# One ring of seven PSUM banks, a step over three quads and new evictors in a windowed-attention backward kernel

## The chip, the cores and the metric

The kernel runs on one core of one Trainium2 chip. The metric is device time in microseconds (us), median of several executions. Executions of one kernel agree within about 0.3%. Runs 1 to 8 were on one chip and 9 to 14 on another; the kernel before took 2572 to 2573 us on both.

PE is TensorE's matmuls, PEld its weight loads, DVE is VectorE, ACT is ScalarE, POOL is GpSimd, SP is SyncE. A "quad" is four tiles of 128 tokens (two 8x8 windows each); there are 128 quads. A "period" is the time between the scores of one quad and of the next.

## The reference, cut

```python
xw  = windows(x)                       # 1024 windows of 64 tokens, C = 384
qkv = xw @ wqkv
p   = softmax(q @ k.T * C ** -0.5)     # 64x64 per window
out = (p @ v) @ wo
# returned: out, and the gradients to x, wqkv, wo for a given grad_out; all bfloat16
```

The kernel folds the weights in pairs first (A, AT for q and k, B, BT for v and wo), so that per quad it needs: two projections z (from grad_out) and y (from x), the scores `sd`, softmax and its backward pass (`Pb`, `Sb`), products u and v, transposes of y and z back to token order (`yq`, `zq`), transposes of Pb and Sb ("turn": `PT`, `ST`), per tile an "attention" of six 64x64-block products (po, pd, pu, pw), and the weight gradients, which sum x-transposed times U and W over all tiles ("GF").

## The kernel before

Every product goes to a PSUM bank and is copied ("evicted") to SBUF by DVE or ACT. Eight banks are in use, in four pools:

```python
ps_pj = tile_pool(name="ps_pj", bufs=2, PSUM)   # z, y, u, v, yz transposes, turns
ps_sd = tile_pool(name="ps_sd", bufs=1, PSUM)   # scores
ps_at = tile_pool(name="ps_at", bufs=4, PSUM)   # po, pd, pu, pw of one attention
ps_dw = tile_pool(name="ps_dw", bufs=1, PSUM)   # a weight gradient, open for 12 matmuls
...
def uv(st, t, part):                            # u: evicted by DVE, v: by ACT
    wgt, dst, cp = ((B_sb, st["uq"], nc.vector.tensor_copy), (AT_sb, st["vq"], nc.scalar.copy))[part]
    pj = ps_pj.tile([P, C], F32, tag="pj")
    for m in range(CK):
        nc.tensor.matmul(pj[:], lhsT=st["xT"][:, t, m, :], rhs=wgt[:, m, :], ...)
    cp(out=dst[:, t, :], in_=pj[:])
...
def attend(st, t):                              # po, pu, pd evicted by ACT, pw by DVE
    both((po, "PT", "uq", True, True), (pd, "Pb", "zq", True, False))
    nc.scalar.copy(out=osb[:], in_=po[:])
    nc.sync.dma_start(out=dram_tile(out_0, bp, t0 + t), in_=osb[:])
    both((pu, "ST", "xq", True, True), (pd, "Sb", "yq", False, False))
    nc.scalar.copy(out=st["Uq"][:, t, :], in_=pu[:])
    both((pw, "Pb", "dq", True, True), (pd, "ST", "vq", False, True))
    nc.vector.tensor_copy(out=st["Wq"][:, t, :], in_=pw[:])
    nc.scalar.copy(out=dsb[:], in_=pd[:])
...
def step(a, b):                 # a: the quad projected now; b: the quad before, attended now
    A(project, 0, 0); A(project, 0, 1); B(0); A(project, 0, 2); A(project, 1, 0); B(1)
    A(project, 1, 1); A(project, 1, 2)
    filler(8)                   # weight-gradient matmuls, one by one
    A(scores); A(soft, 0); A(soft, 1)
    filler(4)
    A(uv, 0, 0); A(uv, 0, 1); A(soft, 2); A(uv, 1, 0); A(uv, 1, 1); A(soft, 3)
    B(2)
    A(uv, 2, 0); A(uv, 2, 1); A(soft, 4); A(uv, 3, 0); A(uv, 3, 1)
    filler(4)
    A(soft, 5)
    for t in range(QUAD):
        A(yz_tok, t, 0); filler(1); A(yz_tok, t, 1); filler(1)
    B(3)
    A(turn, 0); A(turn, 1)
```

PE, DVE and ACT execute in this program order; SP and POOL (the DMA queues) are placed by the scheduler.

Of the kernel before, what the change touches and what calls it, by code (L numbers as in the profile page):

```python
# [9 lines left out]
ALU = mybir.AluOpType  # L10
# [8 lines left out]
MANUAL = {mybir.EngineType.PE, mybir.EngineType.DVE, mybir.EngineType.Activation}  # L19
# [3 lines left out]
def kernel(  # L23
# [36 lines left out]
    ps_pj = ctx.enter_context(tc.tile_pool(name="ps_pj", bufs=2, space=bass.MemoryType.PSUM))  # L60
    ps_sd = ctx.enter_context(tc.tile_pool(name="ps_sd", bufs=1, space=bass.MemoryType.PSUM))
    ps_at = ctx.enter_context(tc.tile_pool(name="ps_at", bufs=4, space=bass.MemoryType.PSUM))
    ps_dw = ctx.enter_context(tc.tile_pool(name="ps_dw", bufs=1, space=bass.MemoryType.PSUM))
# [10 lines left out]
    for jm in range(JK):  # L74
        pt = ps_pj.tile([P, C], BF16, tag="pj")
        for m in range(CK):
            nc.tensor.transpose(pt[:, m * P:(m + 1) * P], w_sb[:, m, jm * P:(jm + 1) * P], ident[:])
        nc.vector.tensor_copy(out=wT_sb[:, jm, :], in_=pt[:])
    woT_sb = const.tile([P, CK, C], BF16)
    for mo in range(CK):  # L80
        pt = ps_pj.tile([P, C], BF16, tag="pj")
# [8 lines left out]
    for dst, left, lo, right, ro, sc in (  # L90
# [5 lines left out]
        for mr in range(CK):  # L96
            pc = ps_pj.tile([P, C], F32, tag="pj")
# [16 lines left out]
    def load(st):  # L114
        bp, t0 = st["at"]
        st["xq"] = xq = grp.tile([P, QUAD, C], BF16, tag="xq", name="xq", bufs=2 * GQ + 3)
        st["dq"] = dq = qp.tile([P, QUAD, C], BF16, tag="dq", name="dq", bufs=4)
# [8 lines left out]

    def project(st, kind, mo):
# [5 lines left out]
        pj = ps_pj.tile([P, QUAD, 2, WT], F32, tag="pj")  # L133
# [3 lines left out]
        if kind == 0:  # L137
            nc.scalar.copy(out=yz[:, mo, :, 0:4:3, :], in_=pj[:])  # L138
            nc.vector.tensor_copy(out=st["zc"][:, mo, :, :, :], in_=yz[:, mo, :, 0:4:3, :])  # L139
        else:  # L140
            nc.scalar.copy(out=yz[:, mo, :, 1:3, :], in_=pj[:])  # L141
# [50 lines left out]
    def uv(st, t, part):  # L192
# [3 lines left out]
        wgt, dst, cp = ((B_sb, st["uq"], nc.vector.tensor_copy), (AT_sb, st["vq"], nc.scalar.copy))[part]  # L196
        pj = ps_pj.tile([P, C], F32, tag="pj")
# [5 lines left out]
    def yz_tok(st, t, part):  # L203
        src, dst = ((st["yz"][:, :, t, 1:3, :], st["yq"]), (st["zc"][:, :, t, :, :], st["zq"]))[part]
        pt = ps_pj.tile([P, CK, P], BF16, tag="pj")
# [4 lines left out]
    def turn(st, kind):  # L210
        src, n = ((st["Pb"], "PT"), (st["Sb"], "ST"))[kind]
        st[n] = dst = qp.tile([P, QUAD, WT], BF16, tag=n, name=n)
        pt = ps_pj.tile([P, QUAD, WT], BF16, tag="pj")
# [5 lines left out]
    def attend(st, t):  # L219
# [4 lines left out]
        po = ps_at.tile([P, C], F32, tag="at", name="po")  # L224
        pd = ps_at.tile([P, C], F32, tag="at", name="pd")
        pu = ps_at.tile([P, C], F32, tag="at", name="pu")
        pw = ps_at.tile([P, C], F32, tag="at", name="pw")
# [8 lines left out]
        nc.scalar.copy(out=osb[:], in_=po[:])  # L236
        nc.sync.dma_start(out=dram_tile(out_0, bp, t0 + t), in_=osb[:])
        both((pu, "ST", "xq", True, True), (pd, "Sb", "yq", False, False))
        nc.scalar.copy(out=st["Uq"][:, t, :], in_=pu[:])  # L239
        both((pw, "Pb", "dq", True, True), (pd, "ST", "vq", False, True))  # L240
        nc.vector.tensor_copy(out=st["Wq"][:, t, :], in_=pw[:])  # L241
        dsb = ob.tile([P, C], BF16, tag="d")
        nc.scalar.copy(out=dsb[:], in_=pd[:])  # L243
        for h, w in ((LO, 1), (HI, 0)):
            nc.gpsimd.dma_start(out=dram_tile(out_1, bp, t0 + t)[WIN * w:WIN * (w + 1)], in_=dsb[h, :])  # L245

    fill = []

    def gf_group(sts):
        def one(f, ma):  # L250
            n = len(sts) * QUAD
            pw = None
            for i in range(n):
                if i == 0:
                    pw = ps_dw.tile([P, C], F32, tag="dw")
                st, t = sts[i // QUAD], i % QUAD
                nc.tensor.matmul(pw[:], lhsT=st["xq"][:, t, ma * P:(ma + 1) * P],  # L257
                                 rhs=st["UW"[f] + "q"][:, t, :], start=(i == 0), stop=(i == n - 1))
                if i == n - 1:
                    nc.vector.tensor_tensor(out=GF_acc[:, f, ma, :], in0=pw[:], in1=GF_acc[:, f, ma, :], op=ALU.add)  # L260
                yield
        for f in range(2):
            for ma in range(CK):
                yield from one(f, ma)
# [9 lines left out]
    def step(a, b):  # L274

        A = (lambda f, *r: f(a, *r)) if a is not None else (lambda f, *r: None)
        B = (lambda t: attend(b, t)) if b is not None else (lambda t: None)
        A(project, 0, 0)
        A(project, 0, 1)
        B(0)  # L280
        A(project, 0, 2)
        A(project, 1, 0)
        B(1)
        A(project, 1, 1)
        A(project, 1, 2)
        filler(8)
        A(scores)
        A(soft, 0)
        A(soft, 1)
        filler(4)  # L290
        A(uv, 0, 0)
        A(uv, 0, 1)
        A(soft, 2)
        A(uv, 1, 0)
        A(uv, 1, 1)
        A(soft, 3)
        B(2)
        A(uv, 2, 0)
        A(uv, 2, 1)
        A(soft, 4)  # L300
        A(uv, 3, 0)
        A(uv, 3, 1)
        filler(4)
        A(soft, 5)
        for t in range(QUAD):
            A(yz_tok, t, 0)
            filler(1)
            A(yz_tok, t, 1)
            filler(1)
        B(3)  # L310
        A(turn, 0)
        A(turn, 1)

    quads = [(bp, t0) for bp in range(NBP) for t0 in range(0, NT, QUAD)]
    sts = [{"at": q, "i": i} for i, q in enumerate(quads)]
    AHEAD = 2
    with tc.manual_schedule(engines=MANUAL):
        for i in range(min(AHEAD, len(sts))):
            load(sts[i])
        held = []  # L320
        for i in range(len(sts) + 1):
            if i + AHEAD < len(sts):
                load(sts[i + AHEAD])
            step(sts[i] if i < len(sts) else None, sts[i - 1] if i else None)
            if i:
                held.append(sts[i - 1])
                sts[i - 1] = None
            if held and (len(held) == GQ or i == len(sts)):
# [6 lines left out]
    for f in range(2):  # L335
        nc.vector.tensor_copy(out=GFb[:, f, :, :], in_=GF_acc[:, f, :, :])
        for mb in range(CK):
            pt = ps_pj.tile([P, C], BF16, tag="pj")
# [53 lines left out]
```

## Time and profile before

| | before |
|---|---|
| time | 2573.8 us |
| period | 19.65 us, 128 of them, plus 59 us of start and end |
| PE / DVE / ACT busy | 90% / 68% / 50% |
| PE idle | 256 us |
| chain of waits: PE / DVE | 47% / 49% |

The page of the kernel before: busy microseconds and share of the span, then the chain that ended last, as shares of the span by engine and by line.

```profile
PE 2318.2 (90%) x22910; PEld 1259.7 (49%) x22910; DVE 1751.3 (68%) x4515; ACT 1295.4 (50%) x2957; POOL 862.0 (33%) x1542
...
DVE 49%; PE 47%; issue 2%; ACT 0%; DMA 0%; SPq 0%; ACTq 0%
```

PE looks full, but the chain runs over DVE for half of its length. The timeline of PE in one period of the kernel before (start, duration, line, tile, count, and in brackets the idle time before it and what ended that):

```profile
1224.80 0.65 PE L199 MATMUL pj<-B_sb,xT 128*128 128x384 bf16 x3
1225.28 0.65 PE L199 MATMUL pj<-AT_sb,xT 128*128 128x384 bf16 x3
1226.50 0.65 PE L199 MATMUL pj<-B_sb,xT 128*128 128x384 bf16 x3 [0.57 <-ACT vq L201]
...
1230.71 0.81 PE L257 MATMUL pw<-Uq,xq 128*128 128x384 bf16 x4
...
1232.60 0.33 PE L207 MATMUL pt<-ident,yz 128*128 128x128 bf16 x3 [0.34 <-DVE yq L208]
...
1235.42 0.29 PE L216 MATMUL pt<-ident,Pb 64*64 64x64 bf16 x8
1235.54 0.30 PE L216 MATMUL pt<-ident,Sb 64*64 64x64 bf16 x8
1236.47 1.46 PE L135 MATMUL pj<-dT,BT_sb 128*128 128x512 bf16 x6 [0.64 <-DVE PT L217]
```

Read the starts, not the durations. The first two u/v products start 0.48 us apart, three matmuls each. The third starts 1.22 us after the second: 0.73 us lost, of which the bracket shows only 0.57, since the modelled end of a matmul lies 0.16 us after the start of the next one. Four such places, and smaller ones, make up the 3 us by which the period exceeds the sum of PE's start-to-start pitches (16.6 us). The Trainium skill ("Perfetto Trace Analysis", Identifying Performance Opportunities) says that the same bubble repeated on the engine that should be saturated can mean that there is not enough SBUF or PSUM for the next tile; here the bubbles repeat in every period.

### The profile page before, as it was taken

Reading aid. Unit: us, or ns where it says so; the run is one execution under the profiler, and the core shown is the slowest. Engines: PE = TensorE matmul, PEld = TensorE weight load, DVE = VectorE, ACT = ScalarE, POOL = GpSimd, SP = SyncE. Lnnn points to the kernel's source line nnn. Section 1 sums busy time; section 2 is a strip of 40 time slices with the busy share of each in tenths; the row PEclk is TensorE's granted clock in tenths of the full one; section 3 lists DMA queues with packets and bytes.
Section 4 is the critical chain, followed back from the end, with each engine's and each line's share of the span. In section 5 each row is a group of like instructions: output and inputs, shape, how many; then the busy total and the mean of one; then the engine's idle time right before and its main releaser. Section 6 shows DMA issues by size and latency. Waiting matters only on the chain.

```text
span 2574.3 us, 59437 instructions
## 1 busy us (share of the span) xinstructions
PE 2318.2 (90%) x22910; PEld 1259.7 (49%) x22910; DVE 1751.3 (68%) x4515; ACT 1295.4 (50%) x2957; POOL 862.0 (33%) x1542
## 2 busy tenths in 40 slices
PE   7899999999999999999999999999999999999997
PEld 4444544444444545444444445444444445454444
DVE  5676677667667766776676677667666766776674
ACT  3545554545555455545455554555454455545552
POOL 2333333333333333333333333333333333333321
PEclk9999999999999999999999999999999999999999
DMA  7455555655555555555555555555555555555531
GB/s 176 101 121 118 122 118 119 129 133 118 118 123 118 121 119 124 115 120 131 129 122 117 122 119 121 121 124 114 124 130 127 121 117 124 116 119 123 122 90 47
DMA packets 624477, 308.61 MB, mean 120 GB/s; under 512 B 458816, under 2 KB 607040, under 8 KB 624192
## 3 DMA queue, kind: packets, MB, share of 16 engines
q1 hardware_dynamic: 550064, 203.49, 37.9%
q0 software_dynamic: 73728, 101.02, 15.4%
q8 instruction: 179, 2.93, 0.5%
q14 instruction: 106, 0.87, 0.1%
q10 hardware_dynamic: 400, 0.29, 0.0%
HBM read 101.84 MB, written 101.84 MB: 79 GB/s over the span
## 4 chain that ended last, share of the span: by engine, by line
DVE 49%; PE 47%; issue 2%; ACT 0%; DMA 0%; SPq 0%; ACTq 0%
PE pj L135 21%; DVE uq L201 10%; PE pw L257 10%; PE pt L207 6%; DVE GF_acc L260 5%; DVE Wq L241 5%; DVE sh L167 4%; DVE mx L162 4%; DVE pr L183 4%; PE sd L149 4%; DVE yq L208 3%; PE po L232 3%; DVE Sb L190 2%; DVE Pb L179 2%; DVE D L185 2%
## 5 line engine op out<-in xcount | busy, mean ns | idle before, releaser
L245 POOL DMA_DIRECT2D out_dram<-dsb x1024 | 586.4, 577 | 1056.1 <-ACT dsb L243 1032.0
L201 ACT CAST vq<-pj 128x384 bf16<-128x384 f32 x512 | 245.3, 479 | 615.9 <-PE pj L199 607.4
L236 ACT CAST osb<-po 128x384 bf16<-128x384 f32 x512 | 255.0, 498 | 508.2 <-PE po L232 500.2
L120 POOL DMA_DIRECT2D dq<-in_grad_out_dram x512 | 276.2, 544 | 624.8 <-PE pt L216 610.6
L199 PEld LDWEIGHTS <-xT 128*128 128x128 bf16 x3072 | 287.5, 97 | 389.7 <-issue 231.7
L199 PE MATMUL pj<-B_sb,xT 128*128 128x384 bf16 x1536 | 333.7, 325 | 93.0 <-ACT vq L201 72.5
L257 PE MATMUL pw<-Wq,xq 128*128 128x384 bf16 x1536 | 384.4, 326 | 2.2 <-DVE GF_acc L260 2.1
L135 PE MATMUL pj<-dT,BT_sb 128*128 128x512 bf16 x1152 | 293.4, 381 | 80.2 <-DVE PT L217 79.9
L257 PEld LDWEIGHTS <-xq 128*128 128x128 bf16 x3072 | 291.0, 98 | 137.2 <-issue 6.3
L162 DVE TENSOR_REDUCE mx<-sd 64x4 f32<-64x256 f32 x256 | 108.2, 422 | 361.7 <-PE sd L149 357.7
L199 PE MATMUL pj<-AT_sb,xT 128*128 128x384 bf16 x1536 | 332.7, 325 | 12.2 <-DVE uq L201 1.1
L257 PE MATMUL pw<-Uq,xq 128*128 128x384 bf16 x1536 | 339.1, 326 | 1.9 <-DVE GF_acc L260 1.9
L139 DVE COPY zc<-yz 128x512 bf16<-128x512 bf16 x384 | 113.1, 295 | 329.2 <-ACT yz L138 329.2
L241 DVE CAST Wq<-pw 128x384 bf16<-128x384 f32 x512 | 283.8, 554 | 18.4 <-PE pw L232 3.6
L135 PE MATMUL pj<-xT,A_sb 128*128 128x512 bf16 x1152 | 291.8, 380 | 0.0
L201 DVE CAST uq<-pj 128x384 bf16<-128x384 f32 x512 | 284.1, 556 | 4.3
L138 ACT CAST yz<-pj 128x512 bf16<-128x512 f32 x384 | 230.4, 600 | 106.4 <-PE pj L135 98.5
L243 ACT CAST dsb<-pd 128x384 bf16<-128x384 f32 x512 | 266.9, 521 | 0.0
L239 ACT CAST Uq<-pu 128x384 bf16<-128x384 f32 x512 | 260.5, 509 | 0.0
L141 ACT CAST yz<-pj 128x512 bf16<-128x512 f32 x384 | 232.9, 677 | 0.4 <-PE pj L135 0.2
L207 PE MATMUL pt<-ident,yz 128*128 128x128 bf16 x1536 | 168.1, 217 | 49.1 <-DVE yq L208 46.9
L208 DVE COPY yq<-pt 128x384 bf16<-128x384 bf16 x512 | 182.0, 356 | 43.1 <-PE pt L207 21.1
(71 smaller groups left out, 3391.1 us busy)
## 6 DMA issues: line engine op xcount, KB each, us to landing
xq<-in_x_dram SPq DMA_DIRECT2D x512, 96.0 KB, 2.9
dq<-in_grad_out_dram POOLq DMA_DIRECT2D x512, 96.0 KB, 2.5
out_dram<-dsb POOLq DMA_DIRECT2D x1024, 48.0 KB, 2.2
out_dram<-osb SPq DMA_DIRECT2D x512, 96.0 KB, 2.8
xT<-xq SPq DMA_TRANSPOSE x128, 3.9
dT<-dq SPq DMA_TRANSPOSE x128, 4.3
w_sb<-in_wqkv_dram SPq DMA_DIRECT2D x1, 864.0 KB, 5.9
out_dram<-dw_sb SPq DMA_DIRECT2D x1, 864.0 KB, 3.8
```

The lines of the kernel that those rows point to most:

```text
L120: nc.gpsimd.dma_start(out=dq[:, t, :], in_=dram_tile(grad_out, bp, t0 + t))
L135: nc.tensor.matmul(pj[:].rearrange("p t w k -> p (t w k)"), lhsT=wgt[:, m, mo * P:(mo + 1) * P], rhs=src[:, :, m, :], start=(m == 0), stop ...
L199: nc.tensor.matmul(pj[:], lhsT=st["xT"][:, t, m, :], rhs=wgt[:, m, :], start=(m == 0), stop=(m == CK - 1))
L201: cp(out=dst[:, t, :], in_=pj[:])
L207: nc.tensor.transpose(pt[:, m, :], src[:, m, :, :].rearrange("p w k -> p (w k)"), ident[:])
L208: nc.vector.tensor_copy(out=dst[:, t, :].rearrange("p (m c) -> p m c", m=CK), in_=pt[:])
L236: nc.scalar.copy(out=osb[:], in_=po[:])
L239: nc.scalar.copy(out=st["Uq"][:, t, :], in_=pu[:])
L241: nc.vector.tensor_copy(out=st["Wq"][:, t, :], in_=pw[:])
L243: nc.scalar.copy(out=dsb[:], in_=pd[:])
L245: nc.gpsimd.dma_start(out=dram_tile(out_1, bp, t0 + t)[WIN * w:WIN * (w + 1)], in_=dsb[h, :])
L257: nc.tensor.matmul(pw[:], lhsT=st["xq"][:, t, ma * P:(ma + 1) * P], rhs=st["UW"[f] + "q"][:, t, :], start=(i == 0), stop=(i == n - 1))
```

## The change

The intent: let no product wait for a bank, give DVE's softmax steps cover, and keep PE in long runs. It has six parts, all in one commit:

1. **Ring.** The pools of two, four and one banks become one pool of seven.
2. **Order.** A step spans three quads: scores and softmax of b, attention of the quad before (c), projection of the quad after (a).
3. **Pairs.** Attentions of tiles 0 and 1 run back to back, so do those of 2 and 3.
4. **Blocks.** Weight gradients run as two blocks of twelve matmuls a step and no longer fill gaps one by one.
5. **Evictors.** u goes from DVE to ACT, U from ACT to DVE, two of three y from ACT to DVE.
6. **Queues.** SP and POOL issue in program order, and grad_out has five buffers instead of four.

```diff
-MANUAL = {PE, DVE, Activation}
+MANUAL = {SP, Pool, PE, DVE, Activation}
-    ps_pj = ... bufs=2   ;   ps_at = ... bufs=4   ;   ps_dw = ... bufs=1
+    ring = ctx.enter_context(tc.tile_pool(name="ring", bufs=7, space=bass.MemoryType.PSUM))
@@ step, cut @@
+        B(scores)
+        B(soft, 0)
+        B(uv, 0, 0)
+        B(uv, 0, 1)
+        B(soft, 1)
+        B(uv, 1, 0)
+        B(uv, 1, 1)
+        B(soft, 2)
+        C_(attend, 0)
+        B(soft, 3)
+        C_(attend, 1)
+        B(soft, 4)
+        filler(1)                      # now a block of twelve matmuls
+        B(uv, 2, 0)
+        B(uv, 2, 1)
+        B(soft, 5)
+        B(uv, 3, 0)
+        B(uv, 3, 1)
+        for t in range(QUAD):
+            B(yz_tok, t, 0)
+            B(yz_tok, t, 1)
+        C_(attend, 2)
+        C_(attend, 3)
+        B(turn, 0)
+        B(turn, 1)
+        for kind in range(2):
+            for mo in range(CK):
+                A(project, kind, mo)
+        filler(1)
+    EV = {"z": "AAA", "y": "DAD", "u": "AAAA", "v": "AAAA", "o": "AAAA", "U": "DDDD", "W": "DDDD", "d": "AAAA"}
... (cut: every pool.tile(...) becomes ring.tile(..., tag="r"); copies go through EV)
```

More of the change, by code (lines that the diff above doesn't have):

```diff
@@ L18 @@
 QUAD = 4
-MANUAL = {mybir.EngineType.PE, mybir.EngineType.DVE, mybir.EngineType.Activation}
+MANUAL = {mybir.EngineType.SP, mybir.EngineType.Pool, mybir.EngineType.PE, mybir.EngineType.DVE, mybir.EngineType.Activation}
 @with_exitstack
@@ L59 @@
     ob = ctx.enter_context(tc.tile_pool(name="ob", bufs=3))
-    ps_pj = ctx.enter_context(tc.tile_pool(name="ps_pj", bufs=2, space=bass.MemoryType.PSUM))
     ps_sd = ctx.enter_context(tc.tile_pool(name="ps_sd", bufs=1, space=bass.MemoryType.PSUM))
-    ps_at = ctx.enter_context(tc.tile_pool(name="ps_at", bufs=4, space=bass.MemoryType.PSUM))
-    ps_dw = ctx.enter_context(tc.tile_pool(name="ps_dw", bufs=1, space=bass.MemoryType.PSUM))
+    ring = ctx.enter_context(tc.tile_pool(name="ring", bufs=7, space=bass.MemoryType.PSUM))
     ident = const.tile([P, P], BF16)
@@ L74 @@
     for jm in range(JK):
-        pt = ps_pj.tile([P, C], BF16, tag="pj")
+        pt = ring.tile([P, C], BF16, tag="r")
         for m in range(CK):
@@ L80 @@
     for mo in range(CK):
-        pt = ps_pj.tile([P, C], BF16, tag="pj")
+        pt = ring.tile([P, C], BF16, tag="r")
         for m in range(CK):
@@ L96 @@
         for mr in range(CK):
-            pc = ps_pj.tile([P, C], F32, tag="pj")
+            pc = ring.tile([P, C], F32, tag="r")
             for mc in range(CK):
@@ L116, in load @@
         st["xq"] = xq = grp.tile([P, QUAD, C], BF16, tag="xq", name="xq", bufs=2 * GQ + 3)
-        st["dq"] = dq = qp.tile([P, QUAD, C], BF16, tag="dq", name="dq", bufs=4)
+        st["dq"] = dq = qp.tile([P, QUAD, C], BF16, tag="dq", name="dq", bufs=5)
         for t in range(QUAD):
@@ L125, in load @@
                                         in_=src[:].rearrange("p t c -> p (t c)"))
+    ENG = {"D": nc.vector.tensor_copy, "A": nc.scalar.copy}
     def project(st, kind, mo):
@@ L132, in project @@
         wgt, src = ((BT_sb, st["dT"]), (A_sb, st["xT"]))[kind]
-        pj = ps_pj.tile([P, QUAD, 2, WT], F32, tag="pj")
+        pj = ring.tile([P, QUAD, 2, WT], F32, tag="r")
         for m in range(CK):
@@ L137, in project @@
         if kind == 0:
-            nc.scalar.copy(out=yz[:, mo, :, 0:4:3, :], in_=pj[:])
+            ENG[EV["z"][mo]](out=yz[:, mo, :, 0:4:3, :], in_=pj[:])
             nc.vector.tensor_copy(out=st["zc"][:, mo, :, :, :], in_=yz[:, mo, :, 0:4:3, :])
         else:
-            nc.scalar.copy(out=yz[:, mo, :, 1:3, :], in_=pj[:])
+            ENG[EV["y"][mo]](out=yz[:, mo, :, 1:3, :], in_=pj[:])
     def scores(st):
@@ L195, in uv @@
                 st[n] = qp.tile([P, QUAD, C], BF16, tag=n, name=n)
-        wgt, dst, cp = ((B_sb, st["uq"], nc.vector.tensor_copy), (AT_sb, st["vq"], nc.scalar.copy))[part]
-        pj = ps_pj.tile([P, C], F32, tag="pj")
+        wgt, dst, cp = ((B_sb, st["uq"], ENG[EV["u"][t]]), (AT_sb, st["vq"], ENG[EV["v"][t]]))[part]
+        pj = ring.tile([P, C], F32, tag="r")
         for m in range(CK):
@@ L204, in yz_tok @@
         src, dst = ((st["yz"][:, :, t, 1:3, :], st["yq"]), (st["zc"][:, :, t, :, :], st["zq"]))[part]
-        pt = ps_pj.tile([P, CK, P], BF16, tag="pj")
+        pt = ring.tile([P, CK, P], BF16, tag="r")
         for m in range(CK):
@@ L212, in turn @@
         st[n] = dst = qp.tile([P, QUAD, WT], BF16, tag=n, name=n)
-        pt = ps_pj.tile([P, QUAD, WT], BF16, tag="pj")
+        pt = ring.tile([P, QUAD, WT], BF16, tag="r")
         for t in range(QUAD):
@@ L223, in attend @@
             st["Wq"] = grp.tile([P, QUAD, C], BF16, tag="Wq", name="Wq")
-        po = ps_at.tile([P, C], F32, tag="at", name="po")
-        pd = ps_at.tile([P, C], F32, tag="at", name="pd")
-        pu = ps_at.tile([P, C], F32, tag="at", name="pu")
-        pw = ps_at.tile([P, C], F32, tag="at", name="pw")
+        po = ring.tile([P, C], F32, tag="r", name="po")
+        pd = ring.tile([P, C], F32, tag="r", name="pd")
+        pu = ring.tile([P, C], F32, tag="r", name="pu")
+        pw = ring.tile([P, C], F32, tag="r", name="pw")
         def both(straight, crossed):
@@ L235, in attend @@
         osb = ob.tile([P, C], BF16, tag="o")
-        nc.scalar.copy(out=osb[:], in_=po[:])
+        ENG[EV["o"][t]](out=osb[:], in_=po[:])
         nc.sync.dma_start(out=dram_tile(out_0, bp, t0 + t), in_=osb[:])
         both((pu, "ST", "xq", True, True), (pd, "Sb", "yq", False, False))
-        nc.scalar.copy(out=st["Uq"][:, t, :], in_=pu[:])
+        ENG[EV["U"][t]](out=st["Uq"][:, t, :], in_=pu[:])
         both((pw, "Pb", "dq", True, True), (pd, "ST", "vq", False, True))
-        nc.vector.tensor_copy(out=st["Wq"][:, t, :], in_=pw[:])
         dsb = ob.tile([P, C], BF16, tag="d")
-        nc.scalar.copy(out=dsb[:], in_=pd[:])
+        ENG[EV["d"][t]](out=dsb[:], in_=pd[:])
         for h, w in ((LO, 1), (HI, 0)):
             nc.gpsimd.dma_start(out=dram_tile(out_1, bp, t0 + t)[WIN * w:WIN * (w + 1)], in_=dsb[h, :])
+        ENG[EV["W"][t]](out=st["Wq"][:, t, :], in_=pw[:])
     fill = []
     def gf_group(sts):
-        def one(f, ma):
-            n = len(sts) * QUAD
-            pw = None
-            for i in range(n):
-                if i == 0:
-                    pw = ps_dw.tile([P, C], F32, tag="dw")
-                st, t = sts[i // QUAD], i % QUAD
-                nc.tensor.matmul(pw[:], lhsT=st["xq"][:, t, ma * P:(ma + 1) * P],
-                                 rhs=st["UW"[f] + "q"][:, t, :], start=(i == 0), stop=(i == n - 1))
-                if i == n - 1:
-                    nc.vector.tensor_tensor(out=GF_acc[:, f, ma, :], in0=pw[:], in1=GF_acc[:, f, ma, :], op=ALU.add)
-                yield
+        n = len(sts) * QUAD
         for f in range(2):
             for ma in range(CK):
-                yield from one(f, ma)
+                pw = ring.tile([P, C], F32, tag="r", name="pg")
+                for i in range(n):
+                    st, t = sts[i // QUAD], i % QUAD
+                    nc.tensor.matmul(pw[:], lhsT=st["xq"][:, t, ma * P:(ma + 1) * P],
+                                     rhs=st["UW"[f] + "q"][:, t, :], start=(i == 0), stop=(i == n - 1))
+                nc.vector.tensor_tensor(out=GF_acc[:, f, ma, :], in0=pw[:], in1=GF_acc[:, f, ma, :], op=ALU.add)
+                yield
     def filler(n):
@@ L272, in filler, with step, on @@
                 fill.pop(0)
-    def step(a, b):
-        A = (lambda f, *r: f(a, *r)) if a is not None else (lambda f, *r: None)
-        B = (lambda t: attend(b, t)) if b is not None else (lambda t: None)
-        A(project, 0, 0)
-        A(project, 0, 1)
-        B(0)
-        A(project, 0, 2)
-        A(project, 1, 0)
-        B(1)
-        A(project, 1, 1)
-        A(project, 1, 2)
-        filler(8)
-        A(scores)
-        A(soft, 0)
-        A(soft, 1)
-        filler(4)
-        A(uv, 0, 0)
-        A(uv, 0, 1)
-        A(soft, 2)
-        A(uv, 1, 0)
-        A(uv, 1, 1)
-        A(soft, 3)
-        B(2)
-        A(uv, 2, 0)
-        A(uv, 2, 1)
-        A(soft, 4)
-        A(uv, 3, 0)
-        A(uv, 3, 1)
-        filler(4)
-        A(soft, 5)
-        for t in range(QUAD):
-            A(yz_tok, t, 0)
-            filler(1)
-            A(yz_tok, t, 1)
-            filler(1)
-        B(3)
-        A(turn, 0)
-        A(turn, 1)
+    def step(c, b, a):
+        def on(st):
+            return (lambda f, *r: f(st, *r)) if st is not None else (lambda f, *r: None)
+        C_, B, A = on(c), on(b), on(a)
+        B(scores)
[16 more added lines that the diff above has]
+        B(uv, 3, 1)
+        for t in range(QUAD):
+            B(yz_tok, t, 0)
[8 more added lines that the diff above has]
+        filler(1)
@@ L314 @@
+    EV = {"z": "AAA", "y": "DAD", "u": "AAAA", "v": "AAAA", "o": "AAAA", "U": "DDDD", "W": "DDDD", "d": "AAAA"}
     quads = [(bp, t0) for bp in range(NBP) for t0 in range(0, NT, QUAD)]
     sts = [{"at": q, "i": i} for i, q in enumerate(quads)]
+    n = len(sts)
     AHEAD = 2
     with tc.manual_schedule(engines=MANUAL):
-        for i in range(min(AHEAD, len(sts))):
+        for i in range(min(AHEAD, n)):
             load(sts[i])
         held = []
-        for i in range(len(sts) + 1):
-            if i + AHEAD < len(sts):
+        get = lambda i: sts[i] if 0 <= i < n else None
+        for i in range(-1, n + 1):
+            if AHEAD <= i + AHEAD < n:
@@ L323 @@
                 load(sts[i + AHEAD])
-            step(sts[i] if i < len(sts) else None, sts[i - 1] if i else None)
-            if i:
+            step(get(i - 1), get(i), get(i + 1))
+            if i > 0:
                 held.append(sts[i - 1])
                 sts[i - 1] = None
-            if held and (len(held) == GQ or i == len(sts)):
+            if held and (len(held) == GQ or i == n):
                 fill.append(gf_group(held))
@@ L337 @@
         for mb in range(CK):
-            pt = ps_pj.tile([P, C], BF16, tag="pj")
+            pt = ring.tile([P, C], BF16, tag="r")
             for ma in range(CK):
@@ L344 @@
         for i, (lhs, f, rhs, r0) in enumerate(((GFT, 0, w_sb, C), (GFb, 0, w_sb, 0), (GFT, 1, woT_sb, 0))):
-            pe = ps_pj.tile([P, C], F32, tag="pj")
+            pe = ring.tile([P, C], F32, tag="r")
             for mb in range(CK):
@@ L355 @@
     for mc in range(CK):
-        pe = ps_pj.tile([P, C], F32, tag="pj")
+        pe = ring.tile([P, C], F32, tag="r")
         for ma in range(CK):
```

## The prediction

> **What bounds it now.** The timeline shows one period of 19.65 us per quad of tiles (128 of them), plus about 60 us of start and end. The page gives PE 90%, DVE 68%, ACT 50% busy, but the Trainium skill ("Trainium Kernel Development and Optimization", Performance Expectations) says that matmul busy time is a bad metric, as matmuls are pipelined. This trace agrees: a 128x384 matmul lasts 325 ns, yet they start 163 ns apart. From start-to-start pitches PE needs per quad: projections 18 x 0.217 = 3.9 us, u/v 3.9, weight gradients 3.9, attention 4 x 0.62 = 2.5, scores 0.70, y/z transposes 1.3, turns 0.25: about 16.6 us. So 3 us (15%) of each period is PE waiting. The chain of waits alternates, PE 47%, DVE 49%: scores -> softmax on DVE -> y/z copies -> turn -> next projection. By the timeline the stalls start-to-start are about 0.7 and 0.25 (u/v for the two "pj" banks, evicted behind exp or softmax work), 0.3 (u), 0.5+0.25 (transposes behind yq), 0.8 (projection behind PT), and about 0.08 at each change between full and 64x64 matmuls.
>
> **What the change does.** The instructions stay the same in number on PE; order and evictors move.
> - Two-deep "pj" + four "at" + one "dw" becomes one ring of 7; 42 allocations per step, exactly six turns. A product waits for the eviction seven products earlier instead of two.
> - Projections of the next quad and one 12-matmul block (3.9 + 1.95 us of PE) stand between turn and the next scores, so PT/ST are needed only by the next step's attention: the 0.8 us wait goes.
> - Four uq evictions move DVE->ACT, four Uq ACT->DVE (DVE about 0.555, ACT about 0.49 us each: nearly neutral), two of three y evictions ACT->DVE. A 128x512 on DVE is estimated at 0.69 us from 0.555 for 384 and its slope. DVE: 13.7 -> about 15 us per quad; ACT: 10.1 -> about 9.
> - SP and Pool issue in program order; loads still lead by over a step, so I expect no cost.
>
> **Walking the new order** with trace durations (DVE pitch 0.47, yq/zq 0.28, ACT 0.375, release to PE 0.05): u/v of t=0,1 unhindered; second attention waits about 0.4 us for osb (behind exp); block 0.1; attentions of t=2,3 about 0.5 in total behind the yq/zq copies; first projection 0.3 behind Wq (DVE backlog of four U/W). Sum about 1.4 us of stalls: period 18.0-18.2 us, DVE then over 80% busy. All 1.5 us is on the critical path, since PE/DVE alternate there.
>
> **Time:** 128 x 18.1 + 60 = about **2375 us** (7.7% less). Eight in ten: 2310 to 2450. Faster by over 2%: 0.90; within 2%: 0.08; slower: 0.02.
>
> **What would show it.** Period 18.1 us in the timeline; PE idle falls from 256 us to about 130; PE matmul durations unchanged; "pj <- PT" waits gone (80 us before), vq waits near zero (72 before), yq waits gone or moved to "po/pd <- zq"; DVE 75-80% of the span or more, ACT about 48%; chain more PE than before (over 60%), DVE share falling. New waits: pw <- ACT osb about 0.4 us a step, pj <- DVE Wq about 0.3.
>
> **What would make it wrong.** DVE is within 10% of PE's need: if its dependent softmax steps or the strided y eviction are slower than estimated, or backlog before the attentions of t=2,3 grows, DVE becomes the limit (19 us). If stalls behind osb cascade through the strict ring order, gain halves. If SP's in-order queue holds output stores behind loads' landings, osb buffers would stall ACT. On the good side, paired attentions may save one mode change each (about 0.15 us) and the walk may be pessimistic (17.3 us, 2275).

## The result

| | before | after |
|---|---|---|
| time (4 runs each) | 2573.8 us | 2294.7 us (2294.0 to 2295.6) |
| ratio, 95% interval | 1 | 0.892 (0.890 to 0.893) |
| period | 19.65 us | 17.59 us |
| start and end | 59 us | 42 us |
| PE idle | 256 us | 62 us |
| DVE / ACT busy per period | 13.5 / 10.0 us | 14.1 / 9.8 us |

A ratio is the mean time of one kernel's fast runs over that of the other's of the same rounds, so not quite the ratio of the medians quoted. Start and end is the span less 128 periods.

The kernel is 10.8% faster: 279 us, where 199 were predicted, and 15 us below the stated range. The page after:

```profile
PE 2231.7 (97%) x22910; PEld 1334.9 (58%) x22910; DVE 1827.0 (80%) x4771; ACT 1259.5 (55%) x2701; POOL 867.2 (38%) x1542
...
PE 95%; ACT 3%; DVE 1%; issue 0%; DMA 0%; ACTq 0%
```

DVE has left the chain although it does more work. The timeline of PE in the changed kernel, over u/v, the two attentions that follow, and then the turns and the projection:

```profile
1210.56 0.65 PE L199 MATMUL pj<-B_sb,xT 128*128 128x384 bf16 x3
1211.05 0.65 PE L199 MATMUL pj<-AT_sb,xT 128*128 128x384 bf16 x3
1211.54 0.65 PE L199 MATMUL pj<-B_sb,xT 128*128 128x384 bf16 x3
1212.02 0.65 PE L199 MATMUL pj<-AT_sb,xT 128*128 128x384 bf16 x3
1212.60 0.35 PE L232 MATMUL po<-uq,PT 64*64 64x384 bf16 x1
...
1213.12 0.32 PE L232 MATMUL po<-uq,PT 64*64 64x384 bf16 x1
...
1213.28 0.32 PE L232 MATMUL pu<-xq,ST 64*64 64x384 bf16 x1
...
1213.93 0.32 PE L232 MATMUL pw<-dq,Pb 64*64 64x384 bf16 x1 [0.32 <-ACT osb L236]
...
1221.07 0.31 PE L216 MATMUL pt<-ident,Pb 64*64 64x64 bf16 x8
1221.36 0.31 PE L216 MATMUL pt<-ident,Sb 64*64 64x64 bf16 x8
1221.61 2.12 PE L135 MATMUL pj<-dT,BT_sb 128*128 128x512 bf16 x9
```

The u/v products now start 0.48 to 0.49 us apart throughout, and the projection behind the turns no longer waits for PT. What is left: the second attention's pw waits for ACT's osb copy, as predicted (0.32 us shown; pw starts 0.65 us after pu instead of 0.16 us, so 0.49 us are lost), and around the second pair PE runs at the pace of DVE's copies, without any bracket to show it: the two turns start 0.29 us apart, against 0.12 us before.

So the mechanism looked right and the size was off by 40%. Whether the stated causes were the causes is what the experiments ask.

### The profile page after: what moved, and what is told of

The parts are those of the page before. It is cut to its first block, busy times and chain, and to the rows that moved or that the text cites. A ratio compares the mean times of both kernels' runs of the same rounds, so it can differ in the third digit from the quotient of the medians.

```text
span 2293.8 us, 59316 instructions
## 1 busy us (share of the span) xinstructions
PE 2231.7 (97%) x22910; PEld 1334.9 (58%) x22910; DVE 1827.0 (80%) x4771; ACT 1259.5 (55%) x2701; POOL 867.2 (38%) x1542
## 4 chain that ended last, share of the span: by engine, by line
PE 95%; ACT 3%; DVE 1%; issue 0%; DMA 0%; ACTq 0%
PE pg L256 22%; PE pj L135 22%; PE pj L199 21%; PE pt L207 7%; PE po L232 5%; PE pw L232 5%; PE sd L149 4%; PE pd L232 3%; PE pu L232 2%; PE pt L216 2%; ACT osb L236 2%; PE pc L97 0%; ACT uq L201 0%; DMA w_sb<-in_wqkv_dram 0%; ACT vq L201 0%
## 5 line engine op out<-in xcount | busy, mean ns | idle before, releaser
L201 ACT CAST uq<-pj 128x384 bf16<-128x384 f32 x512 | 245.3, 479 | 635.1 <-PE pj L199 632.9
L239 DVE CAST Uq<-pu 128x384 bf16<-128x384 f32 x512 | 280.9, 549 | 80.2 <-PE pu L232 80.2
L138 ACT CAST yz<-pj 128x512 bf16<-128x512 f32 x384 | 225.1, 586 | 97.3 <-PE pj L135 81.6
L258 DVE TENSOR_TENSOR GF_acc<-pg,GF_acc 128x384 f32<-128x384 f32 x258 | 143.8, 557 | 167.7 <-PE pg L256 163.8
L256 PE MATMUL pg<-Uq,xq 128*128 128x384 bf16 x1536 | 271.2, 327 | 0.0
L256 PE MATMUL pg<-Wq,xq 128*128 128x384 bf16 x1536 | 270.5, 326 | 0.0
L141 DVE CAST yz<-pj 128x512 bf16<-128x512 f32 x256 | 175.9, 687 | 55.4 <-PE pj L135 55.4
L232 PE MATMUL pw<-dq,Pb 64*64 64x384 bf16 x1024 | 179.7, 330 | 40.0 <-ACT osb L236 40.0
L232 PEld LDWEIGHTS <-ST 64*64 64x64 bf16 x2048 | 147.6, 104 | 113.0 <-issue 102.0
L232 PE MATMUL po<-uq,PT 64*64 64x384 bf16 x1024 | 203.5, 337 | 0.2
```

The source lines that it names most:

```text
L138: ENG[EV["z"][mo]](out=yz[:, mo, :, 0:4:3, :], in_=pj[:])
L232: nc.tensor.matmul(dst[o, :], lhsT=st[lhs][h, t, :], rhs=st[rhs][h, t, :], start=first, stop=last)
L239: ENG[EV["U"][t]](out=st["Uq"][:, t, :], in_=pu[:])
L256: nc.tensor.matmul(pw[:], lhsT=st["xq"][:, t, ma * P:(ma + 1) * P], rhs=st["UW"[f] + "q"][:, t, :], start=(i == 0), stop=(i == n - 1))
```

## The experiments

Two theories. **Ring:** waits for banks made PE and DVE alternate; more depth is the gain, and the new order matters little. **Order** (the prediction's): projections and a block between the turns and the next scores remove the wait for PT and give cover; the ring only helps. For the 80 us by which the prediction was too slow: the banks are not taken in rotation, against mere over-estimates. Every run gave a correct result, with an interval of about 0.2% around its ratio.

### 1. The new order with the old banks

```diff
 # on the changed kernel
-    ring = tile_pool(name="ring", bufs=7, PSUM)
+    ps_pj = tile_pool(bufs=2) ; ps_at = tile_pool(bufs=4) ; ps_dw = tile_pool(bufs=1)
```

> The changed kernel (its order, evictors, twelve-matmul blocks) with the three old groups of banks (two, four, one) in place of the ring. If the ring carries the gain: u/v, y/z transposes and projections again wait for a bank two products back; the y/z pairs alone, no longer interleaved with weight-gradient matmuls, would need about 0.77 us a pair (read from the first steps of the kernel before) against 0.33, so about +1.8 us a period, with u/v about +1, projections +0.5: period about 20.5 to 21.5 us, 2680 to 2800 us, slower than the kernel before. If the order carries the gain: under 2400 us.

Measured 2887.3 us, 12.2% slower than the kernel before (period 22.13 us). PE's timeline in it, where the transposes and an attention follow each other:

```profile
1222.40 0.33 PE L209 MATMUL pt<-ident,zc 128*128 128x128 bf16 x3 [0.16 <-DVE zq L210]
1223.18 0.33 PE L209 MATMUL pt<-ident,zc 128*128 128x128 bf16 x3 [0.16 <-DVE zq L210]
1223.95 0.33 PE L209 MATMUL pt<-ident,zc 128*128 128x128 bf16 x3 [0.16 <-DVE zq L210]
1225.19 0.32 PE L234 MATMUL po<-uq,PT 64*64 64x384 bf16 x1 [0.30 <-ACT osb L238]
1227.25 2.29 PE L137 MATMUL pj<-dT,BT_sb 128*128 128x512 bf16 x9 [0.79 <-DVE PT L219]
```

A pair of transposes takes 0.78 us, as read beforehand; and the projection still waits for PT, 0.79 us, in the very order that was to take this wait away. The change without its ring is a loss of 314 us, 87 us more than the upper end of what was expected. Put the other way round, the ring added last is worth 593 us (2887.3 to 2294.7).

### 2. The old order with the ring

```diff
 # on the kernel before: ps_pj (2), ps_at (4), ps_dw (1) all become
+    ring = tile_pool(name="ring", bufs=7, PSUM)
```

> The kernel before with one ring of seven banks and nothing else. If the ring carries the gain: the bank waits of the kernel before (about 0.7+0.25+0.3 on u/v, 0.75 on transposes, 0.8 on the projection behind PT) go, period 17.3 to 18.2 us, 2280 to 2390 us. If both are needed: the alternation of PE and DVE in the chain stays, period 18.5 to 19.5 us, 2430 to 2560 us.

Measured 2327.9 us (ratio 0.905, period 17.77 us): the ring alone gives 246 of the 279 us. Its page:

```profile
PE 2262.4 (97%) x22910; PEld 1264.6 (54%) x22910; DVE 1664.1 (72%) x4515; ACT 1294.5 (56%) x2957; POOL 876.3 (38%) x1542
...
PE 53%; DVE 43%; issue 2%; ACT 0%; DMA 0%; SPq 0%; ACTq 0%
```

PE's timeline at the place where the kernel before waits for PT, the two turns and the projection behind them:

```profile
1209.41 0.31 PE L214 MATMUL pt<-ident,Pb 64*64 64x64 bf16 x8
1209.67 0.31 PE L214 MATMUL pt<-ident,Sb 64*64 64x64 bf16 x8
1209.92 1.47 PE L133 MATMUL pj<-dT,BT_sb 128*128 128x512 bf16 x6
```

The projection starts 0.25 us after the second turn, before DVE begins the PT copy at 1210.47 us: with another bank to take, it needs nothing of PT. The chain still alternates, yet PE is busy 97% of a much shorter span. The order theory falls. (PE busy at 97% is no floor either, as run 5 shows.)

### 3. Strict rotation of the seven banks

```diff
 # on the changed kernel
+    ring_pool = tile_pool(name="ring", bufs=1, PSUM)
+    def tile(shape, dtype, ...):          # seven tags of one bank each, in turn
+        ring.n += 1
+        return ring_pool.tile(shape, dtype, tag=f"r{ring.n % 7}")
```

> The changed kernel with seven single banks used in strict rotation, as the prediction assumed. In the built program the pool hands out banks out of turn (the last attention's pd takes the bank of the previous attention's po, which ScalarE empties early, where rotation gives it one behind the yq/zq copies). If that is where 0.2 us a period of the unpredicted gain comes from: period about 17.8 us, 2315 to 2330 us, with the first projection of a step about 0.2 us later after the scores start than the 11.75 us of the changed kernel. Rival (the choice of bank is nothing, the walk only over-estimated copies and gaps): 2290 to 2300 us.

Measured 2320.0 us (0.902), period 17.8 us. The pool of the changed kernel does not rotate; it seems to give out the bank that the builder expects to be free first, as far as the built program shows. Banks of the last two attentions and the turns of one period:

```
po:1 pd:3 pu:5 pw:6    po:2 pd:1 pu:7 pw:4    turns 3, 5    z: 2 6 1
```

The last pd takes bank 1 from the previous po, which ACT empties at once; rotation would give it a bank behind DVE's yq copies. Under rotation the first projection starts 11.96 us after the scores instead of 11.75 us, and says why:

```profile
1216.98 2.10 PE L144 MATMUL rt<-dT,BT_sb 128*128 128x512 bf16 x9 [0.15 <-DVE Wq L254]
```

This is the wait "pj behind Wq" of the prediction, which the changed kernel does not have. Strict rotation, the prediction's assumption, costs 25 us.

### 4. The old evictors in the new order

```diff
-    EV = {"y": "DAD", "u": "AAAA", "U": "DDDD", ...}
+    EV = {"y": "AAA", "u": "DDDD", "U": "AAAA", ...}
```

> The changed kernel with the evictors of the kernel before (u on VectorE, U and all y on ScalarE). VectorE falls by about 1.4 us a period, ScalarE rises by as much. If VectorE's load is what paces the last two attentions: about the same or faster, 2260 to 2300 us. If the mapping was part of the gain (u copies on VectorE delay the softmax steps in its in-order queue): 2310 to 2360 us.

Measured 2330.9 us (0.906): the mapping is worth 36 us here, though it adds work to DVE.

### 5. The new evictors in the old order

```diff
 # on run 2: u to ACT, U to DVE, y 0 and y 2 to DVE
```

> The kernel before with the ring of seven and the evictors of the changed kernel (u on ScalarE, U on VectorE, two of three y on VectorE), in the old order. It completes a square of order and evictors, all with the ring: old/old 2328 us, new/old 2331 us, new/new 2295 us. If the evictors alone are worth their 36 us anywhere: about 2290 us, and the new order is worth nothing. If the new order is what makes them pay (u copies no longer stand between softmax steps, projections follow in one run): 2320 us or more.

Neither expectation holds: 2211.9 us (0.860), 83 us faster than the whole change. Its page:

```profile
PE 2185.8 (99%) x22910; PEld 1256.8 (57%) x22910; DVE 1840.9 (83%) x4771; ACT 1211.1 (55%) x2701; POOL 871.6 (39%) x1542
...
PE 97%; DVE 2%; issue 0%; DMA 0%; SPq 0%; ACT 0%
```

The square of order and evictors, all with the ring, in us:

| | old evictors | new evictors |
|---|---|---|
| old order | 2327.9 | 2211.9 |
| new order | 2330.9 | 2294.7 |

(The new-order row also has the new queues; run 7 and run 11 take those apart.) DVE's timeline tells why the evictors pay in the old order. With the old ones (run 2), four u copies stand among the softmax steps:

```profile
1218.36 0.87 DVE L165 TENSOR_TENSOR sh<-sd,mx 64x256 f32<-64x256 f32 x2
1219.26 0.56 DVE L258 TENSOR_TENSOR GF_acc<-pw,GF_acc 128x384 f32<-128x384 f32 x1
1219.74 1.01 DVE L199 CAST uq<-pj 128x384 bf16<-128x384 f32 x2
1220.66 0.41 DVE L173 TENSOR_REDUCE rs<-ex 128x4 f32<-128x256 f32 x1
```

With the new ones (run 5) they are gone:

```profile
1207.74 0.87 DVE L165 TENSOR_TENSOR sh<-sd,mx 64x256 f32<-64x256 f32 x2
1208.65 0.56 DVE L258 TENSOR_TENSOR GF_acc<-pw,GF_acc 128x384 f32<-128x384 f32 x1
1209.29 0.42 DVE L173 TENSOR_REDUCE rs<-ex 128x4 f32<-128x256 f32 x1
```

From sh to rs is 2.30 us in the first, 1.55 us in the second. U copies replace u copies one for one, but they come due at other places: two of four beside the projections, where DVE otherwise waits for the next scores (2.8 us idle there in run 2, 1.3 us in run 5). DVE has more to do in total and the kernel is faster, so the total did not decide; by these timelines it is what stands in the in-order queue between the steps of the chain. The moves of u, U and y were made together, and no run takes them apart.

### 6. A ring of five

```diff
-    ring = tile_pool(name="ring", bufs=7, PSUM)
+    ring = tile_pool(name="ring", bufs=5, PSUM)
```

> The changed kernel with a ring of five banks. If depth is what lets PE ride over the copies that VectorE does late: the attention pairs (four banks at once) wait for the copies of the pair before and the transposes for copies five back; about 1 to 2 us more a period, 2420 to 2560 us. If sharing alone (no group of banks idle while another is short) were enough: under 2340 us.

Measured 2424.6 us (0.943), period 18.6 us. Depth counts, not sharing alone: two banks less cost 130 us. But sharing counts for more: five shared banks are 463 us faster than seven in fixed groups (run 1, 2887.3 us).

### 7. The old queues in the new order

```diff
-MANUAL = {SP, Pool, PE, DVE, Activation}   # and five dq buffers
+MANUAL = {PE, DVE, Activation}             # and four
```

> The changed kernel without its change of the DMA queues: SyncE and GpSimdE left to the scheduler and four dq buffers, as before. Loads lead by more than a period in both, so no change: 2285 to 2305 us. If the gain partly came from there: over 2320 us, with PE waiting for dT or xT.

A miss: 2378.6 us (0.924), 84 us slower. Not dT or xT is waited for, but the output stores. The waits that are new or have grown, with total us, times and the longest (in the changed kernel the first is 10.9 us in total, and the others are not there):

```profile
ACT osb L236 <- DMA out_dram<-osb: 68.6, 39, 5.9
...
PE pj L135 <- ACT osb L236: 39.0, 18, 5.8
PE pj L135 <- DMA out_dram<-osb: 25.4, 22, 3.3
```

The period is the same 17.59 us where nothing happens, but in every third period ACT waits for an osb buffer whose store has not landed, its bank stays full, and the projection stops with it; these 41 periods take 18.1 to 26.3 us and hold 83 us, all of the loss. SyncE's queue in the trace fits: under the scheduler it issues ten loads and transposes in a row between two stores once in three periods, in program order six (in run 5, the old order under the scheduler, eight, without a cost). The prediction named this risk for the changed kernel; the kernel with the scheduler's placement has it. How much of the cure is program order and how much the fifth buffer was not tried.

### 8. Less for DVE in the new order

```diff
-        B(soft, 2); C_(attend, 0)
+        C_(attend, 0); B(soft, 2)          # exp behind the first attention's copies
-    EV = {..., "W": "DDDD"}                # yq, zq all on DVE
+    EV = {..., "W": "DADA", "q": ("DDDD", "DAAD")}   # two zq and two W copies on ACT
```

> The changed kernel with two of eight zq copies and two of four Wq copies moved from VectorE to ScalarE, and exp behind the first attention's two ScalarE copies. If PE's remaining waits (about 0.5 us for osb behind exp, 0.7 us behind VectorE's yq/zq/U/W backlog) are what is left: the period falls from 17.59 to 16.8 to 17.1 us, 2190 to 2235 us. If those waits only moved elsewhere (later Sb, later projection evictions): 2280 us or more.

Measured 2219.5 us (0.863), period 17.0 us. The timelines say where the 75 us were: the first pair of attentions, from its first matmul to the block behind it, takes 1.31 us instead of 1.61 us (the wait for osb behind exp, on ACT), and the second pair with the turns 1.77 us instead of 2.05 us (copies that DVE was late with). The remaining stretches of the period are the same within 0.01 us, so each of the two waits holds about half. Busy time per engine in one period of the changed kernel and then in this one (span, PE, PEld, DVE, ACT; behind them POOL, clock and DMA):

```profile
1204.02:1221.61 17.59, 17.27 (x183) 10.33 (x179) 14.14 (x38) 9.78 (x22) 6.78 (x13) 1.00 0.60 136
```

```profile
1197.91:1214.92 17.01, 16.96 (x178) 10.32 (x179) 12.81 (x34) 11.26 (x26) 6.66 (x13) 1.00 0.68 140
```

### 9. and 10. What of the new order costs: blocks or pairs?

Run 9 gives the second block back as single matmuls between the transposes; run 10 takes the fastest kernel so far (run 5) and pairs its first two attentions.

```diff
 # 9, on the changed kernel
         for t in range(QUAD):
-            B(yz_tok, t, 0); B(yz_tok, t, 1)
+            B(yz_tok, t, 0); filler(1); B(yz_tok, t, 1); filler(1)    # one matmul each
...
-        filler(1)                                                     # a block, after the projections
+        filler(4)                                                     # four matmuls
```

> The changed kernel with its second weight-gradient block given back as single matmuls: one behind each of the eight transposes, four behind the projections; the first block stays. The old order loses nothing there because eight matmuls between the transposes give VectorE time for the yq/zq copies. If the backlog of those copies in front of the last two attentions is what the new order loses (about 0.7 us a period): period about 17.0 to 17.2 us, 2210 to 2250 us. If the pairing of attentions (eight banks in a burst) is the loss: over 2270 us.

```diff
 # 10, on run 5
-        A(project, 0, 1); B(0); A(project, 0, 2); A(project, 1, 0); B(1); A(project, 1, 1)
+        A(project, 0, 1); A(project, 0, 2); B(0); B(1); A(project, 1, 0); A(project, 1, 1)
```

> The old order with the ring and the new evictors (2212 us, period 16.89 us), its first two attentions set side by side between the z and the y projections. In the traces a lone attention takes 0.62 us plus 0.08 us of gap before it, the first of a pair 0.52 us: a pair saves about 0.18 us. If nothing waits for banks: period about 16.7 us, 2185 to 2195 us. If eight banks in a burst cost more than that: 2215 us or more.

Measured 2306.4 us (0.897) and 2236.9 us (0.870). Spreading cost 12 us, and the pair cost 25 us where it was to save 23. In run 9 the second pair has no late yq or zq before it any more, and waits for itself:

```profile
1208.42 0.32 PE L232 MATMUL po<-uq,PT 64*64 64x384 bf16 x1
...
1208.89 0.32 PE L232 MATMUL pu<-xq,ST 64*64 64x384 bf16 x1
...
1209.27 0.31 PE L216 MATMUL pt<-ident,Pb 64*64 64x64 bf16 x8
1209.55 0.31 PE L216 MATMUL pt<-ident,Sb 64*64 64x64 bf16 x8
```

In the pair's second attention pu starts 0.47 us after po, against 0.16 us unhindered, and a turn takes 0.28 us instead of 0.12. An unhindered pair wants eight banks within about 1.1 us (an estimate, twice the 0.52 us from po to po); emptying them takes DVE four copies at 0.47 us start to start. The Trainium skill ("TensorEngine Tiling (Array Packing)", PSUM Bottleneck) says that tiling speeds up TensorE but not PSUM evacuation; this case agrees as to evacuation, 1.1 us of products against 1.9 us of copies; no run here goes without tiling. Run 9 has a second new wait: the scores come only four matmuls behind the last projection and take 0.95 us instead of 0.70, waiting for the last y copy.

### 11. The new queues in the old order

```diff
 # on run 5
-MANUAL = {PE, DVE, Activation}
+MANUAL = {SP, Pool, PE, DVE, Activation}
```

> The old order with the ring and the new evictors, SyncE and GpSimdE in program order as in the changed kernel. In the new order the scheduler's placement of the output stores cost 84 us (ScalarE waited for osb stores). If that cost belongs to the new order alone: 2205 to 2220 us. If program order of the queues is better in general: under 2200 us.

Measured 2206.8 us (0.858), the fastest of all kernels tried, 5 us below run 5. The period is 16.89 us in both; the 5 us are the start, where the first projection begins at 16.6 us instead of 21.6 us. The old order needs the queue change hardly at all; the new order needs it for 84 us. With ring, evictors and queues equal (only the fifth dq buffer differs), the new order costs 2294.7 - 2206.8 = 88 us.

### 12. Everything at once in the new order

```diff
 # on run 9: run 8's mapping and exp, and
-        B(scores); B(soft, 0); B(uv, 0, 0); B(uv, 0, 1)
+        B(uv, 0, 0); B(uv, 0, 1); B(scores); B(soft, 0)
```

> The new order with the lighter VectorE mapping, the spread weight gradients and the first u/v pair ahead of the scores (so that the last y eviction is done when the scores start). If PE's own pitches are then the only limit: period 16.4 to 16.7 us, 2140 to 2180 us, faster than any kernel so far. If one of the moves makes a new wait: 2200 us or more.

A miss: 2264.1 us (0.880), slower than run 8 alone. The scores no longer wait, but the pairs wait for banks as in run 9, and the first block waits for a U copy:

```profile
1213.37 2.11 PE L256 MATMUL pg<-Wq,xq 128*128 128x384 bf16 x12 [0.18 <-DVE Uq L239]
```

Gains in this schedule do not add up.

### 13. and 14. Attentions apart

```diff
 # 13, on the changed kernel; 14, on run 9
-        B(soft, 3); C_(attend, 1); B(soft, 4); filler(block)
+        B(soft, 3); filler(block); C_(attend, 1); B(soft, 4)
-        C_(attend, 2); C_(attend, 3); B(turn, 0); B(turn, 1)
-        project z (3), project y (3)
+        C_(attend, 2); B(turn, 0); B(turn, 1)
+        project z (3); C_(attend, 3); project y (3)
```

> The changed kernel with its attentions apart: the first weight-gradient block stands between the first two, the turns and the z projections between the last two. If the pairs are what the new order loses (eight banks wanted within 1.1 us from a ring of seven, while the eight copies take ScalarE and VectorE about 1.9 us), that costs 0.36 us of mode changes a period and saves about 1 us of waits: 16.8 to 17.1 us, 2190 to 2235 us. If the copies' backlog behind the unspread transposes is the loss: 2270 us or more.

> The same, with the second weight-gradient block spread as in spread_gf. If both backlogs count once the pairs are gone: 2180 to 2205 us, as the old order with the same evictors and queues (2207 us); if only the pairs counted: equal to unpaired within 10 us, or slower by the 0.25 us a period that the scores waited for the last y eviction in spread_gf (32 us).

Measured 2349.9 us (0.914) and 2247.4 us (0.874). Apart without spreading is worse than the change, another miss. The waits have gone to the transposes and what follows them:

```profile
1210.78 0.33 PE L207 MATMUL pt<-ident,yz 128*128 128x128 bf16 x3
1211.38 0.33 PE L207 MATMUL pt<-ident,zc 128*128 128x128 bf16 x3 [0.27 <-DVE yq L208]
1211.64 0.34 PE L232 MATMUL po<-uq,PT 64*64 64x384 bf16 x1
1211.91 0.35 PE L232 MATMUL pd<-zq,Pb 64*64 64x384 bf16 x2
1212.17 0.32 PE L232 MATMUL pu<-xq,ST 64*64 64x384 bf16 x1
```

Each 0.26 us step there is the pitch of one yq/zq copy on DVE. In run 13 DVE waits for the block and for the second attention before it can go on with softmax, so that Sb and the copies come later. With the transposes spread as well (run 14) both waits are gone, and 47 us of the 88 come back; neither expectation of run 14 held (2180 to 2205 us, or no better than run 13). Of the rest, the scores take 0.95 us again: 0.25 us x 128 = 32 us. This last wait is not in the changed kernel, whose second block stands before the scores (0.70 us): spreading the block uncovers them. So pairs and unspread transposes cost together at least 47 us that the old order does not pay, though each taken back alone made the kernel slower. That the step over three quads by itself costs hardly anything is an estimate from what is left, 88 - 47 - 32 = 9 us; no run isolates it. One more thing stays open: every edit also changes which banks the builder picks, and strict-rotation twins of runs 9 to 14 were not made.

### All runs

| run | us | ratio to before |
|---|---|---|
| before | 2573 | 1 |
| new order, old banks (1) | 2887.3 | 1.122 |
| ring of five (6) | 2424.6 | 0.943 |
| old queues (7) | 2378.6 | 0.924 |
| apart, not spread (13) | 2349.9 | 0.914 |
| old evictors (4) | 2330.9 | 0.906 |
| ring alone (2) | 2327.9 | 0.905 |
| strict rotation (3) | 2320.0 | 0.902 |
| spread (9) | 2306.4 | 0.897 |
| **the change** | 2294.7 | 0.892 |
| all at once (12) | 2264.1 | 0.880 |
| apart and spread (14) | 2247.4 | 0.874 |
| old order, ring, new evictors, one pair (10) | 2236.9 | 0.870 |
| less for DVE (8) | 2219.5 | 0.863 |
| old order, ring, new evictors (5) | 2211.9 | 0.860 |
| the same with new queues (11) | 2206.8 | 0.858 |

## Why the prediction was wrong

The direction was right, and so was the reading of the profile: 3 us of PE waiting in each period, behind banks and behind DVE. The time was 80 us too high, outside the range. Three terms make this up, 25, 18 and 37 us, each larger than the 15 us by which the range was missed. Two further steps were wrong as causes, without showing in the number.

- **The step that failed first is "A product waits for the eviction seven products earlier".** The pool does not rotate (banks in the built program, run 3). Run 3, which does rotate, takes 2320.0 us: 25 of the 80 us. The predicted wait of the first projection behind Wq exists in run 3 and not in the changed kernel.
- **Start and end** were carried over as 60 us and measured 42 us: 18 us. The first projection starts at 17.2 us instead of 21.2 us, and the first quads and the tail are shorter. The earlier start takes the ring and the queues together. With the ring alone (run 2) the weight folding ends some 5 us earlier, but the projection then waits 5.59 us for dT and starts at 21.4 us; with the new queues and the old banks (run 1) it starts at 20.2 us.
- **The walk's terms** make up the rest, 37 us or 0.3 us a period. As written, they do not even add up to the 18.1 us used: PE's needs give 16.45 us and the stalls 1.3 us, together 17.75 us. The 0.35 us more stand for no term (the changes between full and 64x64 matmuls, 0.08 us each, are named but not counted), and 17.75 us is close to what strict rotation measured, 17.80 us. "Attention 4 x 0.62" holds for a lone attention; the first of a pair takes 0.52 us (from po to po in the timeline after). yq/zq copies came at 0.265 us, not 0.28, eight of them. So that agreement is partly luck: terms too large stand against changes not counted. These are readings of the trace; no run isolates them.
- **"Projections ... stand between turn and the next scores ...: the 0.8 us wait goes" is wrong as a cause.** With the old banks the new order still waits 0.79 us for PT (run 1); with the ring the old order does not wait for it (run 2). The ring did this, and 246 of the 279 us with it, if it is added first. The prediction had read the wait by the name of its releaser (the copy to PT) and took it for a wait for data that a later use would hide; it was a wait for the bank, which only another bank can end.
- **"Nearly neutral", of the evictors, is wrong.** In the new order they are worth 36 us, in the old order 116 us. The estimate of their work was fair (DVE 14.1 us a period against "about 15"); where in DVE's queue a copy stands was not counted.
- **"Loads still lead by over a step, so I expect no cost"** is right for the change as made, but the queue change is no bystander: without it (and the fifth buffer) the new order takes 84 us more (run 7), and it has a part in the earlier start. The risk named at the end, stores held up until osb buffers run out, is what happens there.
- **What was expected of the profile** held in kind: vq and PT waits gone, pw behind osb 0.32 us a step, DVE 80%, chain 95% PE. PE idle fell to 62 us, not 130, and ACT is at 55%, not 48% (9.8 us of a shorter period, against "about 9").
- **"On the good side, paired attentions may save one mode change each"** holds for the matmuls' pitch, and pairs were a loss nevertheless in the one place where they alone were changed: 25 us (run 10), through the banks.

Where the gain went that the new order should have brought: it was turned into new waits. At equal ring, evictors and queues the new order is 88 us slower than the old. It bunches the copies: eight transposes without matmuls between them, then two attentions, then turns, while the old order puts matmuls that need no new bank between them. Run 14, which takes most of the bunching back, shows this for 47 of the 88 us; for the rest it is argued.

## What to carry to other kernels

Undo each part of a change in which several parts came together: here one part (the ring) gave 246 of the 279 us by itself, one (the evictors) was worth three times as much without another (the order), and the best kernel is the change without its largest piece of new code (the order). Weigh a move of copies between engines by what they stand in front of in the in-order queue, not by the sum of busy times. Matmuls that accumulate into one open bank can serve as filler between products that each need a fresh one, but what this is worth depends on what stands next to it: spread between the transposes they saved 102 us where the attentions stood apart (run 13 to 14) and cost 12 us where they stood in pairs (run 9). A shared pool is worth trying before a new order: all eight banks were in use before and after.

## What the Trainium skill lacked or had wrong

- "Trainium Kernel Development and Optimization", Performance Expectations, says that matmul busy time is a bad metric and weight-load busy share a good one. Confirmed in part: PE busy is 97% at 2327.9 us and 97% at 2294.7 us, and there were 5% to be had from the first. But the weight-load share is 58% after and 57% in run 5, which is 83 us faster, so it did not rank these kernels either (where 64x64 products wait, their loads overlap less and count as more busy time: 194 us in the attention's line after, 135 us in run 5, for the same 6144 loads with a mean of 104 and 105 ns). The page names MFU as well, which for equal work is the time itself.
- "TensorEngine Tiling (Array Packing)", Key Properties, says that changing the tiling mode drains TensorE and gives no figure. Here an attention starts 0.08 us later than the pitch before it asks, and the full-size matmul after it 0.10 us later: about 0.18 us for a lone attention.
- "Perfetto Trace Analysis", Matmuls, says that independent matmul groups should rotate through different PSUM banks. This holds (246 us). The page also asks, under Matmul Optimizations, for all eight banks to be used, but the kernel before did use all eight, and the 246 us came from sharing seven of them instead of keeping them in groups of two, four and one. No page says that; nor what depth is worth when the evicting engines also run a dependent chain (a ring of five gave 2424.6 us, of seven 2294.7 us), nor that strict rotation can be worse than taking what is free: 2320.0 us.
- No page says that queued output stores can stop matmuls by way of SBUF output buffers, an evicting engine and its banks (run 7: 84 us).
